# ScalarE in written order for the whole kernel, with some chunks of a fused attention and SwiGLU kernel placed anew

## The chip, the cores and the metric

The kernel runs on one core of a Trainium2 chip. A core has engines that run side by side, each with its own queue of instructions: TensorE (PE in the profile) multiplies matrices, and its weight loads are listed apart as PEld; VectorE (DVE) and ScalarE (ACT) do elementwise work; GpSimd (POOL) copies and issues transfers here; SyncE (SP) issues transfers. Matmul results land in an on-chip memory called PSUM, in banks, and VectorE or ScalarE takes them from there to the larger on-chip memory, SBUF. Engines meet at semaphores: an instruction waits until what it reads has been written, and until the buffer that it writes has been read by its last user.

The metric is the device time of one execution in microseconds (us); lower is better.

## The reference

Four batches, 8 heads, 768 positions in 8 blocks of 96, head size 64. A small matrix per head (8 by 8) is normalised over rows and columns five times and mixes the blocks of keys and values; each block of queries attends to one mixed block. The result, as 3072 tokens of 512, goes through a SwiGLU layer of width 1536.

```python
P = sort_net
for _ in range(5):
    P = np.exp(P - np.max(P, axis=-1, keepdims=True))
    P = P / (np.sum(P, axis=-1, keepdims=True) + 1e-09)
    P = P / (np.sum(P, axis=-2, keepdims=True) + 1e-09)
k_sorted = np.einsum('bhij,bhjcd->bhicd', P, k_b)
v_sorted = np.einsum('bhij,bhjcd->bhicd', P, v_b)
scores = scale * np.matmul(q_b, k_sb.transpose(0, 1, 2, 4, 3))
attn = softmax(scores)
x = np.matmul(attn, v_sb)        # then (3072, 512)
g = x @ w_gate
out = (g / (1 + np.exp(-g)) * (x @ w_val)) @ w_out
```

## The kernel before

**The layer.** The 3072 tokens are eight tiles of 384: tile `n` is half `n % 2` of batch `n // 2`. For a tile, `ffn(n)` lists twelve pairs of steps `m`. `gate(n, m)` (L406) is four matmuls into a PSUM bank `g_ps` (L410), then a tanh on ScalarE into `th_sb` (L418), then `gs_sb = (th + 1) * g` on VectorE (L420). `value(n, m)` (L424) is four matmuls into `v_ps` (L428), then `h = 0.5 * v * gs` on VectorE (L433). Tanh stands for the sigmoid. Between these, at fixed places, stand the output steps of the tile before: `outp(n - 1, t3, part)` is four matmuls per part into `o_ps` (L445); after part 2 ScalarE copies `o_ps` to `o_sb` (L450) and SyncE sends it out (L452).

**The attention.** A unit is half of the blocks of two heads; a batch has eight units (0 to 3 feed the batch's first tile, 4 to 7 its second). `scores` is sixteen small matmuls into a two-bank PSUM buffer `qk` (L332), `exps` one exp on ScalarE into `e_all` (L345), `av` eight matmuls (L359) followed on VectorE by a reciprocal `r_sb` (L363) and a product `st` (L365). `x_dma` (L391) transposes `st` by a transfer on SyncE's queue into `xt`, the layer's input. Units go in pairs: `units` (L572) puts at a place `at` the scores and the exp of the first unit and the scores of the second; at `at + 1.3` the exp of the second; the two `av` at the places `avs` after `at` (1.9 and 3.6 if nothing else is said; 1.3 and 2.6 for the first half of batch 1).

**Mixing.** `kq_chunk` (L263) mixes keys and queries: matmuls into `tkq` (L269), then a copy to `kqt`. `v_chunk` (L293) does it for values (matmuls L300 into `tv`, copy to `vt`); `v_pair_chunk` (L304) for the values of batches 2 and 3. `drain` (L245) makes the copy on VectorE ("v", L247) or on ScalarE ("s", L249). `kqs` (L588) places pairs of chunks: one through buffer "b" drained by VectorE, one through "a" drained by ScalarE. `vs` (L592) places the four value chunks of batch 1, through the buffers b, a, b, a; their drains are s, s, s, v.

**PSUM.** Two two-bank buffers, tagged "a" and "b", one of each: scores, `av` and the chunks share them, the first unit of a pair in "b" and the second in "a". Three banks tagged "gen" go round among `g_ps`, `v_ps` and the `o_ps` of the first two tiles. One bank tagged "x" holds the other `o_ps`.

**Order.** `merge(main, side)` (L599) walks through the layer's steps, adds up their written costs (0.65 for a gate or value step, 0.87 for a part of an output step) and puts in every side step whose place has been reached. So a side step stands behind the step of the layer that carries the sum past its place. Places in the order listed below are these sums. Up to L568 PE, GpSimd, VectorE and ScalarE keep the order in which the program is written. From L569 on PE and GpSimd do (`manual_schedule`), and a planner that works at compile time with its own estimates orders VectorE, ScalarE and SyncE.

The written order at the two stretches that the change touches, before it (a comma is a new step):

- Tile 1 from place 3.9: g(1,3), v(1,3), value chunk 0, g(1,4), v(1,4), value chunk 1, g(1,5), v(1,5), key and query chunks 2, g(1,6), v(1,6), value chunk 2, g(1,7), v(1,7), value chunk 3, o(0,0) part 0, scores and exp of unit 0 and scores of unit 1, o(0,0) part 1, o(0,0) part 2 with its copy, exp of unit 1, av of unit 0, g(1,8), av of unit 1, v(1,8).
- Tile 3 from place 8.5, for batch 2: g(3,5), v(3,5), scores and exp of unit 0 and scores of unit 1, g(3,6), v(3,6), exp of unit 1, av 0, g(3,7), v(3,7), o(2,1) part 0, av 1, o(2,1) part 1, scores and exp of unit 2 and scores of unit 3, o(2,1) part 2 with its copy, exp of unit 3, g(3,8), av 2, v(3,8), g(3,9), v(3,9), av 3, g(3,10).

Of the kernel before, what the change touches and what calls it, by code (L numbers as in the profile page):

```python
# [17 lines left out]
def kernel(  # L18
# [134 lines left out]
    ET = mybir.EngineType  # L153
    man = tc.manual_schedule(engines={ET.PE, ET.Pool, ET.DVE, ET.Activation})
# [90 lines left out]
    def drain(eng, dst, src):  # L245
        if eng == "v":
            nc.vector.tensor_copy(dst, src)  # L247
        else:
            nc.scalar.copy(dst, src)  # L249
# [13 lines left out]
    def kq_chunk(b, at, n, eng, tag):  # L263
        dst = kqt_tile(b)[:, 0:2 * GI * C].rearrange("p (n c) -> p n c", c=C)
        rm = rmix[b].rearrange("p a (g two) i -> p two (a g) i", two=2)
        tp = chunk_tile("tkq", n // 8, tag).rearrange("p (l n) -> p l n", n=2 * GI)
        for lc in range(n):
            for two in range(2):
                nc.tensor.matmul(tp[two * D:(two + 1) * D, lc, :],  # L269
                                 lhsT=kq_at(b, at + lc),  # L270
                                 rhs=rm[:, two], start=True, stop=True)
        drain(eng, dst[:, :, at:at + n], tp.transpose([0, 2, 1]))
# [45 lines left out]
    def scores(b, u, tag):  # L318
        half, g = divmod(u, H2)
        k_sb, k_at, q_sb, q_at = ((kqts[b], 0, kqts[b], GI * C) if b < 2 else  # L320
                                  (kqts["p"], (b - 2) * GI * C, kqts["q"], (b - 2) * GI * C))
        if tag == "gen":
            wide = None
            pss = [bank_tile("qk"), bank_tile("qk")]
        else:
            wide = pair_tile("qk", tag).rearrange("p (two n) -> p two n", two=2)
            pss = [wide[:, 0], wide[:, 1]]
        for i4 in range(4):
            at = (g * NB + half * 4 + i4) * C
            for two in range(2):  # L330
                lo = two * D
                nc.tensor.matmul(pss[two][:, i4 * C:(i4 + 1) * C],  # L332
                                 lhsT=k_sb[lo:lo + D, k_at + at:k_at + at + 128],
                                 rhs=q_sb[lo:lo + D, q_at + at:q_at + at + C],
                                 start=True, stop=True)
        return wide, pss

    def exps(b, u, wide, pss):
        n = ecount[0] % 8
        ecount[0] += 2  # L340
        if wide is None:
            for two in range(2):
                nc.scalar.activation(e_all[:, n + two, 0:4 * C], pss[two][0:C, 0:4 * C], AF.Exp, scale=scale)
        else:
            nc.scalar.activation(e_all[:, n:n + 2, 0:4 * C], wide[0:C, :, 0:4 * C], AF.Exp, scale=scale)  # L345
        es[(b, u)] = [e_all[:, n, :], e_all[:, n + 1, :]]

    def qk(b, u, tag="b"):
        exps(b, u, *scores(b, u, tag))

    def av(b, u, tag="a"):
        half, g = divmod(u, H2)
        vt = vts[b // 2][:, b % 2].rearrange("p (h i) e -> p h i e", h=H)
        av_ps = pair_tile("av_ps", tag).rearrange("p (two n) -> p two n", two=2)
        o = av_ps.rearrange("p two (i e) -> p two i e", i=4)
        for two in range(2):
            e = es[(b, u)][two]
            for i4 in range(4):
                nc.tensor.matmul(o[:, two, i4, 0:D + 1], lhsT=e[:, i4 * C:i4 * C + 128],  # L359
                                 rhs=vt[:, 2 * g + two, half * 4 + i4, 0:D + 1],  # L360
                                 start=True, stop=True)
        r_sb = ssp.tile([C, 2, 4, 1], FP32, name="r_sb", tag="r")
        nc.vector.reciprocal(r_sb, o[0:C, :, :, D:D + 1])  # L363
        st = ssp.tile([C, 4, 2, D], BF16, name="st", tag="st")
        nc.vector.tensor_tensor(st.rearrange("p i two d -> p two i d"), o[0:C, :, :, 0:D],  # L365
                                r_sb.to_broadcast([C, 2, 4, D]), op=ALU.mult)
        sts[(b, u)] = st
# [11 lines left out]
    def xtr(b, u):  # L379
        half, g = divmod(u, H2)  # L380
        if g == 0:
            xts[(b, half)] = xtp.tile([128, H2, TW], BF16, name=f"xt{b}_{half}", tag="xt")
        x_ps = xt_tile("x", 1)[:, 0]
        x_to(x_ps, b, u)
        return xts[(b, half)][:, g, :], x_ps.rearrange("p a b -> p (a b)")

    def x_dma(b, u):
        half, g = divmod(u, H2)
        if g == 0:
            xts[(b, half)] = xtp.tile([128, H2, TW], BF16, name=f"xt{b}_{half}", tag="xt")  # L390
        nc.sync.dma_start_transpose(out=xts[(b, half)][:, g, :].rearrange("p (i c) -> p i c", c=C),  # L391
                                    in_=sts.pop((b, u)).rearrange("p i two d -> p (i two d)"))
# [13 lines left out]
    def gate(n, m):  # L406
        xt = xts[divmod(n, 2)]
        g_ps = psum.tile([128, TW], FP32, name="g_ps", tag="gen", bufs=3)
        for kc in range(NKC):
            nc.tensor.matmul(g_ps, lhsT=wg_sb[:, kc, ts(m, 128)], rhs=xt[:, kc, :],  # L410
                             start=(kc == 0), stop=(kc == NKC - 1))
        gate_out(n, m, g_ps)
# [153 lines left out]
    gate_out(0, 1, first[2])  # L566
    nc.vector.tensor_copy(rmix[1][lowr, 1].rearrange("p h i -> p (h i)"), ident[lowr, lowr])
    man.__exit__(None, None, None)  # L568
    man = tc.manual_schedule(engines={ET.PE, ET.Pool})  # L569
    man.__enter__()  # L570

    def units(b, us, ats, avs=(1.9, 3.6), lag=3.1):  # L572
        us = list(us)
        todo = []
        for n, at in enumerate(ats):
            u, u2 = us[2 * n:2 * n + 2]
            held = []
            todo.append((at, lambda u=u, u2=u2, held=held: (qk(b, u, "b"), held.append(scores(b, u2, "a")))))
            todo.append((at + 1.3, lambda u2=u2, held=held: exps(b, u2, *held[0])))
            for w, tag, t in ((u, "b", avs[0]), (u2, "a", avs[1])):  # L580
                if b == 0:
                    todo.append((at + t, lambda w=w, tag=tag: av(b, w, tag)))
                    todo.append((at + t + lag, lambda w=w: drain("v", *xtr(b, w))))
                else:
                    todo.append((at + t, lambda w=w, tag=tag: (av(b, w, tag), x_dma(b, w))))
        return todo

    def kqs(b, ats):  # L588
        return [(at, lambda n=n: (kq_chunk(b, n * 32, 16, "v", "b"), kq_chunk(b, n * 32 + 16, 16, "s", "a")))
                for n, at in enumerate(ats)]  # L590

    def vs(f, size, ats):  # L592
        return [(at, lambda m=m: f(1, m * size, size, "sssv"[m], "ba"[m % 2])) for m, at in enumerate(ats)]

    def v_pairs(ats):
        return [(at, lambda m=m: (v_pair_chunk(1, m * 16, 8, "v", "b"), v_pair_chunk(1, m * 16 + 8, 8, "s", "a")))
                for m, at in ats]

    def merge(main, side):  # L599
        done, k = 0.0, 0  # L600
        side = sorted(side, key=lambda t: t[0])
        for c, f in main:
            f()
            done += c
            while k < len(side) and side[k][0] <= done:
                side[k][1]()
                k += 1
        while k < len(side):
            side[k][1]()
            k += 1  # L610

    def ffn(n):
        todo = []
        for m in range(NFC):
            if n > 0 or m > 1:
                todo.append((0.65, lambda m=m: gate(n, m)))
            if n > 0 or m > 0:
                todo.append((0.65, lambda m=m: value(n, m)))
            ends = (7, 9, 11) if n == 1 else (3, 7, 11)
            if n > 0 and m in ends:  # L620
                for part in range(3):
                    todo.append((0.87, lambda t3=ends.index(m), part=part: outp(n - 1, t3, part)))
        return todo
# [7 lines left out]
    def q0_rest():  # L631
        q0_chunk(1, 0, 16, "s", "b")
        q0_chunk(1, 16, 8, "v", "a")

    merge(ffn(0), [(0.0, q0_rest)] + units(0, range(4, 8), (2.0, 6.6)))
    merge(ffn(1), kqs(1, (0.6, 3.3, 7.8)) + vs(v_chunk, 16, (5.2, 6.5, 9.1, 10.4))
          + units(1, range(4), (11.0, 15.6), (1.3, 2.6)))
    hold = const.tile([1, 1], BF16)
    nc.gpsimd.tensor_copy(hold, xts[(1, 0)][0:1, H2 - 1, 0:1])
# [2 lines left out]
    for s in range(4):  # L642
# [1 line left out]
    nc.vector.memset(kqt_tile("p")[:, 2 * GI * C:], 0.0)  # L644
    merge(ffn(2), units(1, range(4, 8), (0.0, 5.5)) + kqs("p", (13.0, 14.7, 20.7)) + v_pairs([(0, 22.5)])
          + [(13.0, lambda: q_dma(2)), (16.4, lambda: q_dma(3))])
    merge(ffn(3), v_pairs([(1, 0.0), (2, 5.1), (3, 6.9)]) + units(2, range(4), (9.8, 14.0)))
    merge(ffn(4), units(2, range(4, 8), (0.0, 8.0)))
    merge(ffn(5), units(3, range(4), (0.0, 8.0)))
    merge(ffn(6), units(3, range(4, 8), (0.0, 8.0)))  # L650
# [36 lines left out]
```

## Time and profile before

Three executions took 247.33, 247.38 and 247.43 us (median 247.38). The profiled execution took 247.53 us; the span from its first to its last instruction is 245.7 us, so 1.83 us lie outside the span.

| stretch (us) | what runs | PE busy | VectorE busy | ScalarE busy |
|---|---|---|---|---|
| 25 to 44 | tile 0, rest of batch 0 | 18.92 | 16.76 | 9.57 |
| 44 to 60 | tile 1, chunks of batch 1 | 15.97 | 11.85 | 9.49 |
| 60 to 78 | tile 1 to 2, first units of batch 1 | 17.04 | 10.19 | 8.27 |
| 78 to 104 | tile 2 | 26.00 | 18.63 | 11.49 |
| 104 to 118 | tile 3, value pairs | 13.87 | 9.55 | 7.57 |
| 118 to 134 | tile 3, first units of batch 2 | 15.82 | 10.78 | 6.81 |
| 134 to 230 | tiles 4 to 7 | 96.00 | 57.46 | 37.79 |
| 230 to 246 | last outputs | 12.36 | 2.94 | 3.38 |

Each row is a window of the profile. The granted TensorE clock is 1.00 in every one. A group of matmuls is read by the distance from its start to the start of the next group, since matmuls overlap at their ends: four gate or value matmuls take 0.65 us so, eight `av` matmuls 0.24, sixteen scores matmuls 0.45, four output matmuls 0.87, sixteen value-chunk matmuls 0.47, sixty-four key and query matmuls 1.13. Where a distance is larger, PE waited.

### The profile page before, as it was taken

The numbers are of one execution on the slowest core, as the hardware profiler recorded it, in microseconds if no ns is written. First come the engines' busy times: TensorE is split into PE (matmuls) and PEld (weight loads), VectorE is DVE, ScalarE is ACT, GpSimd is POOL, SyncE is SP. The second block draws the span as 40 slices with busy tenths as digits, with TensorE's granted clock in tenths as the row PEclk, the third lists the DMA queues.
The fourth block names the chain that finished last, engine by engine and source line by source line (L and its number), as shares of the span: only waits on it lengthen the run. The fifth ranks groups of instructions, "written<-read, shape, count | busy, mean of one in ns | idle before, by whom it ended". The sixth has DMA issues, their size and how long they took to land.

```text
span 245.7 us, 6163 instructions
## 1 busy us (share of the span) xinstructions
PE 237.1 (97%) x2617; PEld 139.4 (57%) x2617; DVE 155.9 (63%) x327; ACT 111.2 (45%) x188; POOL 51.3 (21%) x45
## 2 busy tenths in 40 slices
PE   7799999998999999999999999999999999999994
PEld 5375666675555565555555655565555555555543
DVE  6786789877564685777655845664675576445700
ACT  3977653465444535365542543265235424332311
POOL 5992139990002059300000000000000000000000
PEclk9999999999999999999999999999999999999999
DMA  5989999999995999510121211112111211110122
GB/s 95 216 121 209 206 213 211 206 213 190 156 131 143 196 136 157 139 43 3 45 75 32 61 59 37 41 53 69 32 43 45 75 36 43 43 43 3 43 85 85
DMA packets 39642, 24.77 MB, mean 101 GB/s; under 512 B 29376, under 2 KB 34368, under 8 KB 39616
## 3 DMA queue, kind: packets, MB, share of 16 engines
q0 software_dynamic: 19632, 14.16, 38.7%
q1 hardware_dynamic: 19840, 10.17, 17.4%
q8 instruction: 20, 0.33, 0.6%
q10 hardware_dynamic: 144, 0.07, 0.1%
q14 instruction: 6, 0.05, 0.1%
HBM read 28.32 MB, written 7.86 MB: 147 GB/s over the span
## 4 chain that ended last, share of the span: by engine, by line
PE 86%; DVE 6%; issue 2%; DMA 2%; ACT 2%; DVEq 0%; POOLq 0%
PE v_ps L428 24%; PE g_ps L410 24%; PE o_ps L445 24%; PE tkq L269 3%; PE av_ps L359 3%; PE qk L332 3%; DMA v<-in_v_dram 2%; DVE st L365 1%; DVE vt L247 1%; DVE gs_sb L420 1%; PE o_ps L461 1%; PE idle_ps L477 1%; DVE h L433 1%; PE tq L279 1%; PE tv L300 1%
## 5 line engine op out<-in xcount | busy, mean ns | idle before, releaser
L420 DVE SCALAR_TENSOR_TENSOR gs_sb<-th_sb,g_ps 128x384 bf16<-128x384 bf16 x96 | 52.9, 551 | 49.5 <-ACT th_sb L418 46.4
L428 PE MATMUL v_ps<-xt,wv_sb 128*128 128x384 bf16 x380 | 77.3, 326 | 0.1
L410 PE MATMUL g_ps<-xt,wg_sb 128*128 128x384 bf16 x376 | 76.6, 325 | 0.2
L418 ACT ACTIVATE th_sb<-g_ps 128x384 bf16<-128x384 f32 x96 | 47.1, 491 | 56.2 <-PE g_ps L410 53.6
L445 PE MATMUL o_ps<-wo,h 128*128 128x512 bf16 x276 | 64.4, 379 | 0.0
L433 DVE SCALAR_TENSOR_TENSOR h<-v_ps,gs_sb 128x384 bf16<-128x384 f32 x96 | 53.3, 556 | 7.6 <-DVE gs_sb L420 0.5
L428 PEld LDWEIGHTS <-wv_sb 128*128 128x128 bf16 x380 | 35.5, 97 | 24.0 <-issue 0.7
L410 PEld LDWEIGHTS <-wg_sb 128*128 128x128 bf16 x376 | 34.8, 97 | 23.7 <-issue 0.6
L445 PEld LDWEIGHTS <-h 128*128 128x128 bf16 x276 | 26.0, 98 | 28.4
L450 ACT COPY o_sb<-o_ps 128x512 f32<-128x512 f32 x23 | 13.5, 586 | 46.0 <-PE o_ps L445 46.0
L148 POOL COPY vch<-v 64x1536 bf16<-64x1536 bf16 (+2 forms) x11 | 28.8, 2658 | 13.3 <-DMA v<-in_v_dram 13.3
L345 ACT ACTIVATE e_all<-qk 96x768 bf16<-96x768 f32 x30 | 22.6, 802 | 8.1 <-PE qk L332 8.1
L365 DVE TENSOR_TENSOR st<-av_ps,r_sb 96x512 bf16<-96x512 f32 x32 | 21.8, 680 | 0.3
L359 PEld LDWEIGHTS <-e_all 96*128 96x128 bf16 x256 | 11.9, 97 | 5.2 <-ACT e_all L345 0.9
L363 DVE RECIPROCAL r_sb<-av_ps 96x8 f32<-96x8 f32 x32 | 6.4, 199 | 11.5 <-PE av_ps L359 11.5
L359 PE MATMUL av_ps<-vt,e_all 96*128 96x65 bf16 x256 | 13.1, 193 | 0.0
L249 ACT CAST vt<-tv 96x1024 bf16<-96x1024 f32 (+1 forms) x10 | 9.1, 923 | 5.6 <-PE tv L310 3.6
L247 DVE CAST vt<-tv 96x1024 bf16<-96x1024 f32 (+1 forms) x8 | 8.6, 1082 | 2.2 <-PE tv L310 1.7
L477 PE MATMUL idle_ps<-warm_sb 128*128 128x512 bf16 x25 | 6.9, 382 | 0.0
L247 DVE COPY oq_v<-o_ps 128x128 f32<-128x128 f32 x1 | 0.3, 293 | 9.3 <-PE o_ps L461 9.3
L395 POOL DMA_DIRECT2D q_scr<-in_q_dram x2 | 5.6, 3178 | 0.0
L146 ACT COPY vch<-v 64x768 bf16<-64x768 bf16 (+1 forms) x4 | 5.5, 1388 | 0.3 <-DMA v<-in_v_dram 0.3
(83 smaller groups left out, 130.2 us busy)
## 6 DMA issues: line engine op xcount, KB each, us to landing
out_dram<-o_sb SPq DMA_DIRECT2D x23, 256.0 KB, 2.0
v<-in_v_dram POOLq DMA_DIRECT2D x4, 384.0 KB, 12.7
wg_sb<-in_moe_w_gate_dram POOLq DMA_DIRECT2D x3, 512.0 KB, 11.4
wv_sb<-in_moe_w_val_dram POOLq DMA_DIRECT2D x3, 512.0 KB, 13.2
wo<-in_moe_w_out_dram POOLq DMA_DIRECT2D x3, 512.0 KB, 16.0
kqp<-in_k_dram POOLq DMA_DIRECT2D x2, 768.0 KB, 10.1
q_scr<-in_q_dram POOLq DMA_DIRECT2D x2, 768.0 KB, 17.8
v<-in_v_dram POOLq DMA_DIRECT2D x2, 768.0 KB, 9.8
```

The lines of the kernel that those rows point to most:

```text
L148: eng.tensor_copy(dst, src.transpose([0, 2, 1]))
L247: nc.vector.tensor_copy(dst, src)
L345: nc.scalar.activation(e_all[:, n:n + 2, 0:4 * C], wide[0:C, :, 0:4 * C], AF.Exp, scale=scale)
L359: nc.tensor.matmul(o[:, two, i4, 0:D + 1], lhsT=e[:, i4 * C:i4 * C + 128], rhs=vt[:, 2 * g + two, half * 4 + i4, 0:D + 1], start=True, sto ...
L365: nc.vector.tensor_tensor(st.rearrange("p i two d -> p two i d"), o[0:C, :, :, 0:D], r_sb.to_broadcast([C, 2, 4, D]), op=ALU.mult)
L410: nc.tensor.matmul(g_ps, lhsT=wg_sb[:, kc, ts(m, 128)], rhs=xt[:, kc, :], start=(kc == 0), stop=(kc == NKC - 1))
L418: nc.scalar.activation(th_sb, g_ps, AF.Tanh, scale=0.5)
L420: nc.vector.scalar_tensor_tensor(gs_sb, th_sb, 1.0, g_ps, op0=ALU.add, op1=ALU.mult)
L428: nc.tensor.matmul(v_ps, lhsT=wv_sb[:, kc, ts(m, 128)], rhs=xt[:, kc, :], start=(kc == 0), stop=(kc == NKC - 1))
L433: nc.vector.scalar_tensor_tensor(h_tiles[n][:, m, :], v_ps, 0.5, gs_tiles.pop(m), op0=ALU.mult, op1=ALU.mult)
L445: nc.tensor.matmul(o_ps, lhsT=h_w[:, m, ts(t3, 128)], rhs=wo_sb[part][:, m % 4, :], start=(m == 0), stop=(m == NFC - 1))
L450: nc.scalar.copy(o_sb, o_ps)
```

## The change

Four edits. ScalarE joins the engines that keep the written order from L569 to the end. Batch 1's last value chunk is drained by ScalarE, where VectorE did it. Batch 1's third key and query chunks and three of its value chunks get other places, by which the written order around them becomes: value chunk 0, g(1,4), value chunk 1, v(1,4), g(1,5), key and query chunks 2, v(1,5), g(1,6), value chunk 2, v(1,6), value chunk 3, g(1,7), v(1,7), o(0,0) part 0, scores of units 0 and 1 as before. The second pair of batch 2 goes from place 14.0 to 14.9, by which it becomes: o(2,1) part 1, o(2,1) part 2 with its copy, scores and exp of unit 2 and scores of unit 3, g(3,8), exp of unit 3, v(3,8), av 2, g(3,9), v(3,9), g(3,10), av 3.

```diff
-    man = tc.manual_schedule(engines={ET.PE, ET.Pool})
+    man = tc.manual_schedule(engines={ET.PE, ET.Pool, ET.Activation})
...
     def vs(f, size, ats):
-        return [(at, lambda m=m: f(1, m * size, size, "sssv"[m], "ba"[m % 2])) for m, at in enumerate(ats)]
+        return [(at, lambda m=m: f(1, m * size, size, "s", "ba"[m % 2])) for m, at in enumerate(ats)]
...
-    merge(ffn(1), kqs(1, (0.6, 3.3, 7.8)) + vs(v_chunk, 16, (5.2, 6.5, 9.1, 10.4))
+    merge(ffn(1), kqs(1, (0.6, 3.3, 7.1)) + vs(v_chunk, 16, (5.2, 5.8, 8.4, 9.1))
           + units(1, range(4), (11.0, 15.6), (1.3, 2.6)))
...
-    merge(ffn(3), v_pairs([(1, 0.0), (2, 5.1), (3, 6.9)]) + units(2, range(4), (9.8, 14.0)))
+    merge(ffn(3), v_pairs([(1, 0.0), (2, 5.1), (3, 6.9)]) + units(2, range(4), (9.8, 14.9)))
```

## The prediction

> **What bounds it now.** I read the page's head and the chain of waits first.
>
> ```profile
> PE 237.1 (97%) x2617; PEld 139.4 (57%) x2617; DVE 155.9 (63%) x327; ACT 111.2 (45%) x188; POOL 51.3 (21%) x45
> PE 86%; DVE 6%; issue 2%; DMA 2%; ACT 2%; DVEq 0%; POOLq 0%
> ```
>
> TensorE sets the end; ScalarE is busy 45% of the time. The change removes no matmul, so it can only take away or add moments at which PE waits. I went through PE's timeline from 25 us on and compared each distance from start to start with the usual one for its kind. Distances up to 0.10 too long come wherever the kind changes, and I leave those. The real waits are few: 0.32 at 43.07, 0.19 at 56.42, 1.13 at 60.45, 0.29 at 108.41, 0.26 at 120.64, 0.25 at 124.27, and some of 0.1. From 131 us to the end there is none above 0.1. So about 2.5 us are to be had, 1% of the span, most of it at 60 and 120.
>
> The timeline of all engines at the first place (start, length, engine, line, names):
>
> ```profile
> 59.02 0.63 PE L300 MATMUL tv<-rmix,vch 128*128 128x64 bf16 x16
> 60.01 0.56 DVE L433 SCALAR_TENSOR_TENSOR h<-v_ps,gs_sb 128x384 bf16<-128x384 f32 x1
> 60.45 0.34 PE L332 MATMUL qk<-kqt 64*128 64x96 bf16 x8
> 60.49 1.21 DVE L247 CAST vt<-tv 96x1024 bf16<-96x1024 f32 x1
> 61.75 0.35 PE L332 MATMUL qk<-kqt 64*128 64x96 bf16 x8 [0.96 <-DVE vt L247]
> 62.03 1.90 PE L445 MATMUL o_ps<-wo,h 128*128 128x512 bf16 x8
> 62.13 0.81 ACT L345 ACTIVATE e_all<-qk 96x768 bf16<-96x768 f32 x1 [0.49 <-PE qk L332]
> 63.97 0.59 ACT L450 COPY o_sb<-o_ps 128x512 f32<-128x512 f32 x1 [1.02 <-PE o_ps L445]
> 64.66 0.41 PE L359 MATMUL av_ps<-vt,e_all 96*128 96x65 bf16 x8
> ```
>
> The last value chunk sits in buffer "a" until VectorE, held by an h, has drained it; the second unit's scores want "a" and wait. And the planner ran the second exp (62.13) before the output copy (63.97), though the copy is written first.
>
> At the second place:
>
> ```profile
> 119.03 1.50 ACT L345 ACTIVATE e_all<-qk 96x768 bf16<-96x768 f32 x2 [0.47 <-PE qk L332]
> 120.43 0.49 ACT L418 ACTIVATE th_sb<-g_ps 128x384 bf16<-128x384 f32 x1
> 120.95 0.55 DVE L420 SCALAR_TENSOR_TENSOR gs_sb<-th_sb,g_ps 128x384 bf16<-128x384 bf16 x1 [1.14 <-ACT th_sb L418]
> 121.55 0.81 PE L428 MATMUL v_ps<-xt,wv_sb 128*128 128x384 bf16 x4
> 123.95 0.69 DVE L365 TENSOR_TENSOR st<-av_ps,r_sb 96x512 bf16<-96x512 f32 x1
> 124.27 0.77 PE L332 MATMUL qk<-kqtq,kqtp 64*128 64x96 bf16 x16
> ```
>
> Two exps in a row hold up a tanh whose matmuls were done at 119.90; its gs ends at 121.50, frees the bank, and v(3,7) starts 0.26 late. At 124.27 the scores wait for the st that empties "a" at 124.64.
>
> **Tile 1's chunks.** The count of instructions stays; one drain goes from VectorE (1.21) to ScalarE (1.01). From g(1,4) at 51.47 I laid out the new order with the usual distances: four gates and values each 0.65, three chunks 0.47, one pair of key and query chunks 1.13 and its 0.09 at the change of kind. That is 7.83, so o(0,0) starts at 59.30 instead of 59.49: **-0.19**. It holds if chunk 2, at 56.41, finds "b" drained. Key and query chunks 2 now start at 53.98; half of their matmuls later (0.57, and 0.1 to the end) VectorE can drain. It has gs(1,5) until 55.14, then the drain of 1.21 ends near 56.3. The cover is 0.1. Behind h(1,5), which is now written after it, it would start at 56.4 and cost 1.3. ScalarE's queue reads: chunk 0 51.67, tanh 52.58, chunk 1 52.98, tanh 54.07, key and query drain 55.23, tanh 56.60, chunk 2 57.07, chunk 3 58.19 to 59.20, tanh(1,7) 59.10. That tanh is 0.26 late, at no cost: its bank is wanted by g(1,8), past 62. The second scores come at 60.48 and find "a" free since 59.20; they take 0.45 in all, not 1.58: **-1.13**, covered by 1.3 us.
>
> **The copy before the second exp.** Strict order puts the exp of unit 1 behind the copy, which waits for all eight output matmuls. Queued behind it are tanh(1,8) and, on PE, the second av. With the o(0,0) start at 62.03 as zero, the copy starts at 1.94. No row has an exp right behind a copy. Low end: a drain and the tanh behind it overlap by 0.10 (49.80 to 50.71), so the exp starts 0.49 after the copy, ends 0.81 later, and the av starts 0.05 after that (19.57 to 19.62): 3.29 instead of 2.63, 0.66. High end: copy to tanh took 0.65 (75.92 to 76.57), 0.82; but that tanh waited for PE. I take **+0.70**. Here a page speaks. By the Trainium skill ("ScalarE: Activation LUTs", "What ACT_TABLE_LOAD costs") activations in a row overlap by about 93 ns, which gives 0.50 between the starts and 0.67 for the term; the 0.65 row above is no test of it. Gs(1,8) then ends 0.6 before v(1,9) needs its bank, so nothing is late next.
>
> **Tile 3.** The tanh overtakes the second exp: it can start at 119.92, gs ends at 120.98, v(3,7) is not held: **-0.26**. The second exp ends at 121.1; its av is at 122.80. Moving the pair behind o(2,1) part 2 puts 0.87 of matmuls before its scores: **-0.25** (nothing to -0.34, with the change of kind). ScalarE then does copy, exp, tanh(3,8), exp: 125.0, 125.6, 126.3, 126.7 on the old clock less the gain; av 2 at 126.62 wants an exp that ends at 126.45. VectorE's work after it I put at 0, between -0.13 (the small wait at 130.24 gone) and +0.77 (below). SyncE's transposes of units 2 and 3 come later against tile 4: the last was issued at 130.53, landed in 2.3, and was wanted at 134.7. 1.9 us of slack shrink to about 0.8.
>
> **Other pairs.** In seven of fourteen pairs a tanh is now written between the exps (two in tile 0, two in tile 3, one each in tiles 4, 5, 6), in one the copy, in six nothing. In the long stretch:
>
> ```profile
> 144.32 1.50 ACT L345 ACTIVATE e_all<-qk 96x768 bf16<-96x768 f32 x2
> 145.79 0.49 ACT L418 ACTIVATE th_sb<-g_ps 128x384 bf16<-128x384 f32 x1
> 147.78 0.41 PE L359 MATMUL av_ps<-vt,e_all 96*128 96x65 bf16 x8
> ```
>
> The tanh cannot start earlier (its matmuls end at 145.75), so the exp ends at 145.79 + 0.39 + 0.81 = 146.99 and the av has 0.8 to spare: 0. Without that cover it would cost up to 1.2 a tile. In tile 0 the second av comes 0.8 and 1.6 after its exp: 0, at best -0.1. A rule speaks against the mixing of functions: the same page ("Table sets: the hidden batching unit") says to group calls by table set and gives about 2.7 us for a switch, 38 us for fourteen. It also lists exp and tanh in one set, and the trace has one table load, 1.28 us, in the whole run, so nothing is added.
>
> **A transfer that does not move along.** Tile 2's last input chunk was issued at 73.37 and landed 2.3 later, at 75.67; g(2,0)'s fourth matmul wanted it at 76.21. Its predecessors were slowed by transfers that end near 69 whatever PE does (the first landed in 6.3). If it stays while PE comes 0.62 earlier, 0.1 is lost; between 0 and 0.6 I take **+0.10**.
>
> **Sum.** -0.19 - 1.13 + 0.70 - 0.26 - 0.25 + 0.10 = -1.03, on the profiled execution's 247.53 us: 246.50. It lies 0.15 above the median of the three, so 246.35, rounded to **246.4**.
>
> **Rivals.**
> - The second exp does not end up behind the copy: no +0.70, 245.7. For it: the planner did put it first. Against it: a fixed order leaves no such choice. Chance 0.10.
> - VectorE in tile 3 is planned badly: r(av 2) before gs(3,8) and st before h(3,8), as in the trace of before (126.94, 127.22, 127.69, 128.29). Then v(3,9) waits 0.34 and g(3,10) 0.43: 247.1. Against it: av 2 is now written behind v(3,8). Chance 0.21.
> - Slower: VectorE drains key and query chunks 2 late. Each us that the drain starts after 55.2 costs PE one at chunk 2. Behind h(1,5) it is +1.3 and 247.6, no change; behind gs(1,6) as well (57.67) the drain ends at 58.8, chunk 2 waits 2.4, and the time is 248.8. It decides from a start at 56.7 on. For it: VectorE's order is planned anew from estimates. Against it: all such drains of before came right behind what is written before them. Chance 0.16 with what else may slow it.
>
> The forecast itself has 0.50, its own range being 246.0 to 246.8, and 0.03 is left for the unnamed. A measurement tells 0.2%, 0.49 us, from no change: faster is below 246.89, slower above 247.87. Faster 0.62, same 0.21, slower 0.17. The range, 245.6 to 247.8, takes in the first two rivals and leaves out the slow one.
>
> **What would show it.** Scores near 60 us without a gap; then a gap of 0.7 before the second av, with the copy before the exp; v(3,7) at the usual distance; no wait before the moved scores; tiles 4 to 7 unchanged to 0.1. A gap before chunk 2, or a wait of v(3,9) for a gs, would make the forecast wrong.

## The result and the profile after

The changed kernel takes 246.16 us (median of four runs, 246.00 to 246.27), the kernel before 247.41 (four runs, 247.33 to 247.60). The ratio is 0.9943, with a 95% interval from 0.9931 to 0.9955: faster by 0.6%. The forecast was 246.4, with 246.0 to 246.8 as its own range. The profiled execution took 246.00 us with a span of 244.2.

The page's head and its chain of waits, after:

```profile
PE 237.1 (97%) x2617; PEld 139.4 (57%) x2617; DVE 154.8 (63%) x326; ACT 112.3 (46%) x189; POOL 51.3 (21%) x45
PE 90%; DVE 4%; DMA 2%; ACT 1%; issue 1%; POOLq 0%
```

TensorE's busy time is what it was. One drain has moved from VectorE to ScalarE (one instruction and 1.1 us less there, one more and 1.1 more here). On the chain TensorE's share rose from 86% to 90%: waits went, not work.

The timeline of the first place, after (all engines; start, length, engine, line, names):

```profile
54.85 1.22 DVE L247 CAST kqt<-tkq 128x1024 bf16<-128x1024 f32 x1
56.19 0.63 PE L300 MATMUL tv<-rmix,vch 128*128 128x64 bf16 x16
56.86 2.12 ACT L249 CAST vt<-tv 96x1024 bf16<-96x1024 f32 x2
57.31 0.63 PE L300 MATMUL tv<-rmix,vch 128*128 128x64 bf16 x16
...
59.08 1.03 PE L445 MATMUL o_ps<-wo,h 128*128 128x512 bf16 x4
60.03 0.51 PE L332 MATMUL qk<-kqt 64*128 64x96 bf16 x16
60.42 0.81 ACT L345 ACTIVATE e_all<-qk 96x768 bf16<-96x768 f32 x1 [1.05 <-PE qk L332]
60.48 1.90 PE L445 MATMUL o_ps<-wo,h 128*128 128x512 bf16 x8
62.22 0.41 PE L359 MATMUL av_ps<-vt,e_all 96*128 96x65 bf16 x8
62.42 0.59 ACT L450 COPY o_sb<-o_ps 128x512 f32<-128x512 f32 x1 [1.19 <-PE o_ps L445]
62.46 0.81 PE L410 MATMUL g_ps<-xt,wg_sb 128*128 128x384 bf16 x4
62.90 0.81 ACT L345 ACTIVATE e_all<-qk 96x768 bf16<-96x768 f32 x1
63.76 0.42 PE L359 MATMUL av_ps<-vt,e_all 96*128 96x65 bf16 x8 [0.49 <-ACT e_all L345]
```

VectorE's drain of key and query chunks 2 ends at 56.07, and value chunk 2 starts at 56.19 without a wait. ScalarE's drains of value chunks 2 and 3 end at 58.98. The sixteen scores matmuls run in one piece, 0.45 us from start to start where it was 1.58. Then the second exp stands behind the copy, and the second av waits for it: from g(1,8) to that av it is 1.30 where four gate matmuls take 0.65.

The second place, after, from the same view:

```profile
119.07 0.49 ACT L418 ACTIVATE th_sb<-g_ps 128x384 bf16<-128x384 f32 x1
119.46 0.80 ACT L345 ACTIVATE e_all<-qk 96x768 bf16<-96x768 f32 x1
119.59 0.55 DVE L420 SCALAR_TENSOR_TENSOR gs_sb<-th_sb,g_ps 128x384 bf16<-128x384 bf16 x1 [0.66 <-ACT th_sb L418]
119.76 0.81 PE L410 MATMUL g_ps<-xt,wg_sb 128*128 128x384 bf16 x4
120.42 0.81 PE L428 MATMUL v_ps<-xt,wv_sb 128*128 128x384 bf16 x4
...
124.00 0.51 PE L332 MATMUL qk<-kqtq,kqtp 64*128 64x96 bf16 x16
124.44 0.82 PE L410 MATMUL g_ps<-xt,wg_sb 128*128 128x384 bf16 x4
```

The tanh now stands before the exp, gs ends at 120.14, and v(3,7) follows g(3,7) at the usual 0.65. The moved scores take 0.45, without a wait.

To see where time goes in each kernel I cut PE's timeline at the same instructions in every trace. The figures are distances between starts, in us; the first stretch begins with the first of the layer's matmuls past 25 us, the last ends with the first matmul of the last output. The runs e1 to e8 are told below.

| stretch | before | after | e1 | e2 | e3 | e4 | e5 | e6 | e7 | e8 |
|---|---|---|---|---|---|---|---|---|---|---|
| tile 0, to the key and query chunks | 18.67 | 18.54 | 18.53 | 18.67 | 18.54 | 18.54 | 18.54 | 18.55 | 18.68 | 18.57 |
| tile 1, to o(0,0) part 0 | 15.45 | 15.27 | 15.45 | 15.26 | 15.26 | 15.26 | 15.85 | 15.27 | 15.26 | 15.27 |
| to v(1,8) | 5.42 | 4.94 | 6.08 | 4.28 | 4.28 | 4.95 | 4.95 | 4.94 | 4.28 | 4.28 |
| to tile 3 | 40.87 | 40.87 | 40.86 | 41.20 | 40.87 | 40.86 | 40.87 | 41.14 | 40.87 | 40.96 |
| tile 3 | 28.47 | 27.84 | 28.25 | 28.66 | 27.84 | 27.84 | 27.84 | 27.84 | 28.67 | 27.84 |
| tiles 4 to 7 | 105.32 | 105.34 | 105.32 | 105.31 | 105.31 | 105.31 | 105.33 | 107.48 | 105.42 | 105.34 |

Before to after, 0.13 comes from tile 0, 0.18 from tile 1's chunks, 0.48 from the stretch behind them and 0.63 from tile 3: 1.42 us. The two profiled executions differ by 1.53; the rest is 0.10 before 25 us, where the change does nothing, and 0.01 of rounding. The medians differ by 1.25.

### The profile page after: what moved, and what is told of

Read it like the earlier page. It is cut to its first block, busy times and chain, and to the rows that moved or that the text cites. A ratio compares the mean times of both kernels' runs of the same rounds, so it can differ in the third digit from the quotient of the medians.

```text
span 244.2 us, 6162 instructions
## 1 busy us (share of the span) xinstructions
PE 237.1 (97%) x2617; PEld 139.4 (57%) x2617; DVE 154.8 (63%) x326; ACT 112.3 (46%) x189; POOL 51.3 (21%) x45
## 4 chain that ended last, share of the span: by engine, by line
PE 90%; DVE 4%; DMA 2%; ACT 1%; issue 1%; POOLq 0%
PE v_ps L428 25%; PE o_ps L445 25%; PE g_ps L410 25%; PE av_ps L359 3%; PE qk L332 3%; PE tkq L269 3%; DMA v<-in_v_dram 2%; PE o_ps L461 1%; PE idle_ps L477 1%; PE tv L300 1%; DVE st L365 1%; DVE vt L247 1%; PE tq L279 1%; PE tv L310 1%; PE g_ps L550 1%
## 5 line engine op out<-in xcount | busy, mean ns | idle before, releaser
L345 ACT ACTIVATE e_all<-qk 96x768 bf16<-96x768 f32 x30 | 23.3, 801 | 4.5 <-PE qk L332 4.5
L249 ACT CAST vt<-tv 96x1024 bf16<-96x1024 f32 (+1 forms) x11 | 10.1, 931 | 4.7 <-PE tv L310 3.6
L247 DVE CAST vt<-tv 96x1024 bf16<-96x1024 f32 (+1 forms) x7 | 7.4, 1064 | 2.2 <-PE tv L310 1.7
L477 PE MATMUL idle_ps<-warm_sb 128*128 128x512 bf16 x25 | 7.6, 411 | 0.0
L247 DVE COPY oq_v<-o_ps 128x128 f32<-128x128 f32 x1 | 0.3, 292 | 9.3 <-PE o_ps L461 9.3
```

## The experiments

Each was timed beside the kernel before, e1 to e4 on one chip (where that takes 247.48 us) and e5 to e8 on another (247.41); ratios are to it. The theory is that of the prediction, a sum of single waits of PE. The first rival is that one edit brings the gain and the others hardly matter.

**e1: the order alone.**

```diff
 (kernel before)
-    man = tc.manual_schedule(engines={ET.PE, ET.Pool})
+    man = tc.manual_schedule(engines={ET.PE, ET.Pool, ET.Activation})
```

> The kernel before with one edit alone: ScalarE in written order; chunks and pairs stay where they were. Theory of the sums: the scores near 60 us still wait 1.1 us for VectorE's drain and chunk 2 still waits 0.2; the second exp behind the copy adds a wait of 0.66; the tanh before the second exp takes 0.26 off at v(3,7); the second pair of batch 2, still at its old place, now has its second exp behind the copy and tanh(3,8) behind both, some 0.3 lost at v(3,9); 0.1 gained in tile 0. In all +0.6: 248.0 us. Rival: the written order is what brings the gain and the places hardly matter: 246.5 or less.

247.81 us against 247.48, ratio 1.0011 (1.0002 to 1.0020): hardly slower, half of the loss that was expected, and not the rival's gain. Tile 1 is as said: the wait at the scores stays and the copy adds 0.66 (6.08 against 5.42). Tile 3 gains 0.22, where I had about nothing. The timeline of this run:

```profile
120.56 0.49 ACT L418 ACTIVATE th_sb<-g_ps 128x384 bf16<-128x384 f32 x1
121.91 0.81 PE L428 MATMUL v_ps<-xt,wv_sb 128*128 128x384 bf16 x4
...
124.11 0.69 DVE L365 TENSOR_TENSOR st<-av_ps,r_sb 96x512 bf16<-96x512 f32 x1
124.63 0.57 PE L332 MATMUL qk<-kqtq,kqtp 64*128 64x96 bf16 x16
125.13 1.04 PE L445 MATMUL o_ps<-wo,h 128*128 128x512 bf16 x4
126.20 0.58 ACT L450 COPY o_sb<-o_ps 128x512 f32<-128x512 f32 x1 [0.38 <-PE o_ps L445]
126.68 0.81 ACT L345 ACTIVATE e_all<-qk 96x768 bf16<-96x768 f32 x1
127.39 0.49 ACT L418 ACTIVATE th_sb<-g_ps 128x384 bf16<-128x384 f32 x1
127.94 0.54 DVE L420 SCALAR_TENSOR_TENSOR gs_sb<-th_sb,g_ps 128x384 bf16<-128x384 bf16 x1
128.53 0.81 PE L428 MATMUL v_ps<-xt,wv_sb 128*128 128x384 bf16 x4 [0.17 <-DVE gs_sb L420]
```

With the tanh first, VectorE's `st` ends 2.89 after the start of v(3,7), not 3.09, and the scores at the old place take 0.50, not 0.70. The wait that I gave to the move of the pair is mostly gone without it. What the old place costs under the written order stands below: the copy, the second exp and tanh(3,8) in a row, and v(3,9) late by 0.33.

**e2: the places alone.**

```diff
 (changed kernel)
-    man = tc.manual_schedule(engines={ET.PE, ET.Pool, ET.Activation})
+    man = tc.manual_schedule(engines={ET.PE, ET.Pool})
```

> The changed kernel with ScalarE left to the planner: the places and the drain of the change alone. Theory of the sums: both waits near 57 and 60 us gone (-1.32), no wait for the second exp since the planner runs it before the copy, -0.25 from the moved pair, the wait of 0.26 at v(3,7) stays, tile 0 as before: 247.4 - 1.57 = 245.85 us, faster than the changed kernel by about 0.3. Rival, that the places need the written order: 246.5 or more.

246.29 us against 247.48, ratio 0.9952 (0.9939 to 0.9964). The gain that was expected for tile 1 came (15.26 and 4.28); the total missed by 0.44, and lies between the two theories. Two stretches were worse than said. In tile 3 the planner puts both exps of the moved pair before tanh(3,8), and v(3,9) waits 0.47: the tile takes 28.66, 0.19 more than before, where -0.25 was expected.

```profile
124.54 1.51 ACT L345 ACTIVATE e_all<-qk 96x768 bf16<-96x768 f32 x2
125.93 0.50 ACT L418 ACTIVATE th_sb<-g_ps 128x384 bf16<-128x384 f32 x1
126.46 0.55 DVE L420 SCALAR_TENSOR_TENSOR gs_sb<-th_sb,g_ps 128x384 bf16<-128x384 bf16 x1 [3.00 <-ACT th_sb L418]
127.07 0.81 PE L428 MATMUL v_ps<-xt,wv_sb 128*128 128x384 bf16 x4 [0.30 <-DVE gs_sb L420]
```

And at the start of tile 2 a transfer came too late, from PE's timeline of this run:

```profile
74.21 0.65 PE L410 MATMUL g_ps<-xt,wg_sb 128*128 128x384 bf16 x3
75.03 0.32 PE L410 MATMUL g_ps<-xt,wg_sb 128*128 128x384 bf16 x1 [0.18 <-DMA xt<-st]
75.29 0.51 PE L332 MATMUL qk<-kqt 64*128 64x96 bf16 x16
```

The fourth matmul starts 0.82 after the first where three take 0.49: 0.33 lost, since the last transposed chunk, issued at 70.87, landed 4.1 later. The profiled execution was the slowest of its five (246.51; the others took 246.20 to 246.32), so this loss may stand in it alone; tile 3's 0.44 is as large as the miss of the median.

**e3: the second exp before the copy.** Two lines of `units` and the call for the first half of batch 1:

```diff
 (changed kernel)
-    def units(b, us, ats, avs=(1.9, 3.6), lag=3.1):
+    def units(b, us, ats, avs=(1.9, 3.6), lag=3.1, second=1.3):
-            todo.append((at + 1.3, lambda u2=u2, held=held: exps(b, u2, *held[0])))
+            todo.append((at + second, lambda u2=u2, held=held: exps(b, u2, *held[0])))
-          + units(1, range(4), (11.0, 15.6), (1.3, 2.6)))
+          + units(1, range(4), (11.0, 15.6), (1.3, 2.6), second=1.1))
```

> The changed kernel with the second exp of batch 1's first pair placed 1.1 instead of 1.3 behind the first, so that it is written before the output copy. Theory: the wait of 0.65 before the second av goes, and nothing else moves: 246.15 - 0.65 = 245.5 us. Rival: what waits next (VectorE's work on the first av, the bank of g(1,8)) takes at least half of it: 245.8 to 246.1.

245.40 us against 247.48, ratio 0.9915 (0.9901 to 0.9928). It beats both kernels: the changed one by 0.76 us by the medians, and in the traces the stretch to v(1,8) is 0.66 shorter. All engines:

```profile
60.39 1.50 ACT L345 ACTIVATE e_all<-qk 96x768 bf16<-96x768 f32 x2 [1.05 <-PE qk L332]
62.38 0.58 ACT L450 COPY o_sb<-o_ps 128x512 f32<-128x512 f32 x1 [0.49 <-PE o_ps L445]
62.43 0.81 PE L410 MATMUL g_ps<-xt,wg_sb 128*128 128x384 bf16 x4
63.08 0.41 PE L359 MATMUL av_ps<-vt,e_all 96*128 96x65 bf16 x8
```

The exps were done at 61.89, in the time in which the copy could only wait. Nothing else took the place of that wait.

**e4: the last value chunk drained by VectorE, in its new place.**

```diff
 (changed kernel)
-        return [(at, lambda m=m: f(1, m * size, size, "s", "ba"[m % 2])) for m, at in enumerate(ats)]
+        return [(at, lambda m=m: f(1, m * size, size, "sssv"[m], "ba"[m % 2])) for m, at in enumerate(ats)]
```

> The changed kernel with the last value chunk of batch 1 drained by VectorE again, in its new place. Theory A, the place does it: the drain now starts about 58.1, behind h(1,6), and ends near 59.3, before the scores want the buffer at 60.25; nothing is lost: 246.15 us, within 0.15. Theory B, the engine does it: the wait of about 1.1 at the scores comes back: 247.2 us.

246.27 us against 247.48, ratio 0.9946 (0.9934 to 0.9959): the same as the changed kernel, 15.26 and 4.95. Theory A holds. The drain ran from 58.22 to 59.43 on VectorE and the scores came at 60.20.

```profile
58.22 1.21 DVE L247 CAST vt<-tv 96x1024 bf16<-96x1024 f32 x1
...
60.20 0.52 PE L332 MATMUL qk<-kqt 64*128 64x96 bf16 x16
```

The new place alone brings the 1.13; in that place the engine of the drain makes no difference. Whether ScalarE's drain at the old place would have brought them too was not run. The trace of before speaks for it:

```profile
58.83 0.49 ACT L418 ACTIVATE th_sb<-g_ps 128x384 bf16<-128x384 f32 x1
60.84 0.81 ACT L345 ACTIVATE e_all<-qk 96x768 bf16<-96x768 f32 x1 [1.51 <-PE qk L332]
```

ScalarE is idle from 59.32. A drain of 1.01 from there would end near 60.3 by my estimate, and the second unit's scores would want the buffer at 60.68, half of the usual 0.45 behind 60.45.

**e5: key and query chunks 2 behind v(1,5).**

```diff
 (changed kernel)
-    merge(ffn(1), kqs(1, (0.6, 3.3, 7.1)) + vs(v_chunk, 16, (5.2, 5.8, 8.4, 9.1))
+    merge(ffn(1), kqs(1, (0.6, 3.3, 7.8)) + vs(v_chunk, 16, (5.2, 5.8, 8.4, 9.1))
```

> The changed kernel with batch 1's third key and query chunks back at place 7.8, behind v(1,5); all else as changed. Theory: their drain on VectorE then stands behind h(1,5), starts near 55.35 and ends at 56.55, while value chunk 2 wants the buffer at 56.17: a wait of 0.4, 246.55 us. It tests whether the cover of 0.1 that the prediction named is real. Rival, that chunk 2 is not held by that drain: no wait, 246.15 us.

246.56 us against 247.41, ratio 0.9966 (0.9954 to 0.9978), 0.40 above the changed kernel; in the trace the stretch grew by 0.58. The drain began at 55.45 and ended at 56.67, and chunk 2 started at 56.71:

```profile
55.45 1.22 DVE L247 CAST kqt<-tkq 128x1024 bf16<-128x1024 f32 x1
56.71 0.63 PE L300 MATMUL tv<-rmix,vch 128*128 128x64 bf16 x16 [0.42 <-DVE kqt L247]
```

So that drain does decide when chunk 2 can start, and an h before it costs at once.

**e6 and e7: the second av of the second pair early in tiles 4 to 6**, once in the changed kernel and once with ScalarE left to the planner:

```diff
 (changed kernel, and e2; the same in tiles 5 and 6)
-    merge(ffn(4), units(2, range(4, 8), (0.0, 8.0)))
+    merge(ffn(4), units(2, range(4, 8), (0.0,)) + units(2, range(6, 8), (8.0,), (1.9, 2.3)))
```

> The changed kernel with the second av of the second pair in tiles 4, 5 and 6 placed 2.3 instead of 3.6 behind the pair, right behind the first av. Theory: in the written order the second exp, behind the tanh, ends 0.55 after that place, so each of the three tiles waits 0.55: +1.65, 247.8 us. It takes away the cover of 0.8 that made the term nothing. Rival, that the tanh in between costs nothing even without it: 246.2 us.

> The same early av in tiles 4 to 6, with ScalarE left to the planner, so that both exps run in a row and the second ends 0.7 before the av. Theory: no wait for the exp; the two products on VectorE now come in a row and may hold a gs, up to 0.3 a tile: 246.3 us to 247.2. If it is as slow as the run with the written order, the wait there is VectorE's and not the exp's.

e6: 248.51 us against 247.41, ratio 1.0059 (1.0036 to 1.0082). e7: 246.43, ratio 0.9957 (0.9946 to 0.9969). Tile 4 of e6, all engines:

```profile
144.48 0.49 ACT L418 ACTIVATE th_sb<-g_ps 128x384 bf16<-128x384 f32 x1 [0.67 <-PE g_ps L410]
144.86 0.80 ACT L345 ACTIVATE e_all<-qk 96x768 bf16<-96x768 f32 x1
144.93 0.41 PE L359 MATMUL av_ps<-vt,e_all 96*128 96x65 bf16 x8
145.72 0.42 PE L359 MATMUL av_ps<-vt,e_all 96*128 96x65 bf16 x8 [0.38 <-ACT e_all L345]
```

The second av starts 0.79 after the first where 0.24 is usual: 0.55 lost, as said, in each of the three tiles, and 0.17 more in each at a later value step (v(4,7) in tile 4), behind VectorE's two products in a row: 2.14 in all. (The 0.27 more before tile 3 are again a transfer that came too late.) In e7 the two av run in one piece and the tiles lose 0.10 together. So the written order does cost when its cover, the time that the av leaves the exp to spare, is taken away.

**e8: the last transpose of tile 0 written earlier**, on top of e3:

```diff
 (e3)
-                    todo.append((at + t + lag, lambda w=w: drain("v", *xtr(b, w))))
+                    todo.append((min(at + t + lag, 12.9), lambda w=w: drain("v", *xtr(b, w))))
```

> The version with the second exp before the copy, and in tile 0 the last transpose of the attention's output written before v(0,11) instead of behind it. Theory: the wait of 0.32 at 43 us, where the fourth matmul of g(1,0) waits for VectorE's copy of that transpose, goes: 245.4 - 0.3 = 245.1 us. Rival: VectorE's planned order is the same as before, with gs(0,11) ahead of that copy, and gs(0,11) waits for a tanh; then little or nothing comes of it: 245.4 us.

245.39 us against 247.41, ratio 0.9917 (0.9904 to 0.9930): no better than e3, as the rival said. But not by the rival's reason: g(1,0) itself no longer waits. The four transposes now wait for their one PSUM bank instead, which VectorE empties only at 42.26; they start at 42.31, `[0.16 <-DVE xt L247]`, 0.97 after the gate step before them, where 0.65 is usual. The same 0.32 is lost one step earlier.

## Why the prediction was right

**What bounds it.** PE, with a few waits: confirmed. The 1.42 us that went are waits at four places.

**Tile 1's chunks.** -0.19 was said, 0.18 came, and e5 shows what the cover of 0.1 guards: VectorE's drain in that order. -1.13 was said for the scores; 1.58 became 0.45. Here the prediction named place and engine together; e4 shows that the place is enough, and ScalarE's drain at the old place was not tried.

**The copy before the second exp.** +0.70 was said, 0.65 measured. ScalarE began the exp 0.48 after the copy, the low end of the two that I had. The Trainium skill ("ScalarE: Activation LUTs", "What ACT_TABLE_LOAD costs") has activations in a row overlap by about 93 ns; here a copy of 0.59 and the exp behind it overlap by about 0.10, which agrees.

**Tile 3.** -0.26 and -0.25 were said, and 0 for VectorE's work behind it, with -0.13 as its good end; 0.63 came, all three. The parts were wrong as single effects: the order alone gives 0.22 (e1), the place alone loses 0.19 (e2). The tanh ahead of the exp frees v(3,7) as said, in e1 too. The -0.25 has the right size for the wrong reason, and that is luck. The order frees VectorE early and removes 0.20 of the wait at the scores by itself (e1), so that 0.05 of it is left for the place. What the place then does is to keep the copy from standing between the second pair's exps, which cost 0.33 at v(3,9) in e1. And the place needs the order, which keeps tanh(3,8) ahead of the second exp: the planner's two exps in a row cost 0.47 at v(3,9) (e2). Only the sum was right.

**The transfer that does not move along.** +0.10 was said; no loss came. The chunk was issued 0.76 earlier than before while PE came 0.89 earlier, which left 0.4 of slack. In e2 it cost 0.33 and in e7, with the same order up to there, nothing; in e6, with the changed kernel's order up to there, 0.27. The row's slack was thin, as said; whether it is used up changed between executions with the same order up to there. Nor did the transfers that slow its predecessors end near 69 whatever PE does: GpSimd's last one ahead of the chunk, into `q_scr`, landed at 71.05 before, 72.94 after, 73.92 in e2 and 72.83 in e7.

**Other pairs.** 0 was said, and tiles 4 to 7 take 105.34 against 105.32. E6 and e7 show that the cover of 0.8 is what makes it nothing. Tile 0 gave 0.13, a little past the good end of what was said (0 to -0.1). It lies at one gate step, which the prediction's list of waits leaves out: before, it starts at 40.07, 0.18 late, behind an h that ends at 40.01; after, at 39.84, 0.05 late, behind that h at 39.78. In the kernels with the written order tile 0 takes 18.53 to 18.55 (18.57 in e8, which moves a transpose there), with the planner 18.67 or 18.68.

**Sum.** -1.03 was said; the stretches of the two profiled executions give -1.42. The 0.4 between them are tile 0 (0.13), the small wait behind tile 3's pair (0.12), the transfer (0.10) and the copy (0.05). The medians differ by 1.25, since the profiled execution of before lay above its median and that of after below.

**The rivals.** That the copy would not stand before the exp is refuted by the trace after. The slow rival, a late drain of key and query chunks 2, did not come about: it ran right behind gs(1,5), at 54.85. Nor did the rival of tile 3, VectorE's work on av 2 ahead of gs(3,8): gs(3,8) starts at 125.83 and the reciprocal at 126.30, and v(3,9) follows g(3,9) by 0.65. The rival of the experiments, that one edit brings the gain, comes near for the places: alone they take 246.29 (e2), with the order 246.16, and the intervals of the two ratios overlap. The order gains 0.13 in tile 0 and 0.82 in tile 3 by the traces of e2 and after, and gives 0.66 of it back behind the copy, which e3 wins again.

## What to carry to other kernels

Where an engine takes its work in a fixed order, look for each instruction that waits long and ask what short work stands behind it: moving one exp ahead of a copy gave 0.76 us by the medians (0.66 in the traces), where the whole change had given 1.25. Terms that share an engine are not to be added as if they stood alone: in tile 3 an order and a place that gained 0.22 and lost 0.19 by themselves gained 0.63 together. When a drain moves to another engine and to another place at once, test each of them alone before either gets the credit.

## What was not expected of the hardware

Of the four transposing transfers on SyncE's queue that feed tile 2, the first two landed 4.2 to 9.2 us after their issue over the ten traces, while other transfers were under way; the four of batch 2's first half, issued from about 121 us on, landed after 2.3 to 2.4 in every one. The last one of tile 2 landed after 2.3 in eight traces, and after 3.5 in e3 and 4.1 in e2, where it was issued 1.3 us or more earlier than in the others. Its arrival is a race with PE that cannot be read from one trace.
